# Attention by hash buckets with an MLP on one core: the first two chunks in a new order, their rows of bits copied without DMA, the dummy products on a constant

## Chip, cores and metric

The kernel runs on one core of one Trainium2 chip. The metric is the device time of one execution in microseconds (us). Before the change three runs took 306.94, 307.81 and 308.57 us; their median is 307.81 us.

## What is computed

Attention over 4 batches, 8 heads, 768 tokens and heads 64 wide, in which a query sees only the keys whose six hash bits equal its own; behind it, on 512 features a token, a norm, an MLP to 2048 and back, and a residual.

```python
B, H, S, D = q.shape                                  # 4, 8, 768, 64, float32
q_bits = (np.einsum('bhsd,dk->bhsk', q, proj) > 0)    # proj: 64 x 6
k_bits = (np.einsum('bhsd,dk->bhsk', k, proj) > 0)
mask = q_bucket[:, :, :, None] == k_bucket[:, :, None, :]   # all six bits equal
scores = np.where(mask, scale * q @ k.T, -1e9)
attn = exp(scores - max) / (sum + 1e-09)
x = (attn @ v)                                        # to [4, 768, 512]
mu, var = mean(x), mean((x - mu) ** 2)
xn = (x - mu) / np.sqrt(var + 1e-06) * g_ln
out = x + np.maximum(xn @ w_ch1, 0.0) @ w_ch2         # 512 x 2048, 2048 x 512
```

## The kernel before

**Work and tiles.** The work is cut into 12 chunks: a batch b and a third t of its tokens, 256 of them. Attention of a chunk is four pairs of heads of three units each. A unit is the scores on TensorE (`sc`, L486), their exponential on ScalarE (`ex`, L492) and the product with the values on TensorE (`av`, L506), which follows a unit or more later; after the third unit of a pair VectorE divides (`rc` and `x`, L534 to L544). The mask needs no step of its own: `slots` holds for each head the transposed tokens in rows 0 to 63 and the hash bits, as plus or minus one half, in rows 64 to 69, and the product over 70 rows is so far down where a bit differs that the exponential vanishes. `vaug` holds the values in bf16 with a column of ones.

Before the first chunk can start, the tokens of batch 0 go through a chain: loads on SyncE's queue (L147, L182), transposes in fp32 on TensorE (`tpose`, L236), their eviction to `qkT` by VectorE or ScalarE (L246, L248, L250), a cast into `slots` (L192 on ScalarE, L196 on VectorE or GpSimd), products with the projection (`hash`, L350 and L373), a comparison on VectorE that leaves `bits` (L355, L380), and the copies of the rows of bits into `slots` by `copy_by` (L189 to L196). A pair of heads has four such copies of 6 partitions x 768 (heads 0 and 1 are done apart, with copies of 6x384). Later batches are prepared otherwise: a cast on GpSimd (`nat`, L269), a DMA that transposes (L293), hashes on blocks (L312) and bits moved by DMA (L325, L331).

The MLP of a chunk is: statistics (`stats`, L564 in the first chunk) and the normed tokens on VectorE (`xn`, L572 in the first chunk, L600 later), transposes of xn on TensorE (`xnTp`, L588) with a copy to `xnT`, the first product (`hp`, L625) with its ReLU by VectorE or ScalarE (`hbuf`, L132 and L136), and the second product (`o`, L647). The weights come by DMA on GpSimd's queue (L671 and L678).

**What sets the order.** The first two chunks, and part of the attention of the third, are written out by hand under a manual schedule: each engine runs its instructions in the order in which `first_two` issues them. It reads the table `FIRST_TWO`, and `ORDER` gives the order of the units. The letters that the change touches:

- `<` is the next unit's scores and exponential, `>` the next unit's product with the values.
- `T h a` with an engine is the transposes of q (a is 0) or k (1) of head h and their eviction by VectorE (V) or ScalarE (A); `C`, `c` and `x` cast one half of the tokens, both, or the other half.
- `h` and `H` are the hash products and the bits; `r` and `B` copy the rows of bits. Of their letters the first four name the engine of each copy: V is VectorE, A ScalarE, G GpSimd, and S a DMA on SyncE's queue.
- `P`, `R` cast the values of a pair and sum them. `v`, `L`, `N`, `V`, `O`, `D`, `K`, `Q` are the loads of batch 1, its casts, its values (cast L408 and sums L415 to L417 on GpSimd), transposes, hashes, blocks and squares.
- `z` and `Z` with a number are so many dummy products of 128x128 on TensorE, whose result nobody reads (`wakep`, L799): `z` in the PSUM pool of `av`, `Z` in the general one.
- `S`, `X`, `Y`, `U` are statistics, norm, transposes and the eight steps of the first product of chunk 0's MLP; `M` is the norm of chunk 1.
- `W0` loads the first weights, `W1` and `W2` the second. `e` loads the gains of the norm (`gbc`, on SyncE), `b` makes the block-diagonal projection by eight small copies on GpSimd (L683), `p` copies the projection.

The dummy products read the tile `wake`, which VectorE clears at the start (L61 and L62). From chunk 2 on a scheduler, `interleave`, mixes the units with fillers: `plan` says which steps of the next batches' preparation come with which chunk, in up to three parts by `|`.

Of the kernel before, what the change touches and what calls it, by code (L numbers as in the profile page):

```python
# [10 lines left out]
BF16 = mybir.dt.bfloat16  # L11
# [17 lines left out]
def kernel(  # L29
# [11 lines left out]
    nc = tc.nc  # L41
    P = 128
# [15 lines left out]
    consts = ctx.enter_context(tc.tile_pool(name="consts", bufs=1))  # L58


    wake = consts.tile([P, P], BF16)  # L61
    nc.vector.memset(wake, 0.0)  # L62
    wake2 = consts.tile([P, 2], BF16)
    nc.vector.memset(wake2, 0.0)

# [682 lines left out]
    FIRST = 6  # L748
    mlp = {n: mlp_steps(*chunks[n], xs[n]) for n in range(2)}

    ORDER = "020 000 0012 0212 01 10 20 30 21 12 31 11"
    FIRST_TWO = """
p Z26 T00A T01Aa h00 C00V h01 C01A T10Aa z3 T11As e h10 r0AVVG P0 C10G C11V h11 r1VVVV < z3 < T20V T30Va < >
T21A T31V >
P1 < < H1 >
c3G >
C20A < R0 W0 T40Vs T41V >
x3V < T50V B1VSVV T51A < C21G C41G >
C40V >
< H2 P3 >  # L760
< c5G T60Va x5G T61A B2VSGS < >
P2 C61G T70V C60G T71Va < C70V >
< H3 C71G >
B3VGVG b < >
>
< R1 >
< >
W1 L0 N00 < >
< >
S0 < W2 v0 >  # L770
< >
V0 < >
S1 X0 X1 Y0V < Y1V >
< N01 U0 L1 >
< >
O0 U1 < < K011 K000 K001 >
U2 K010 Q011 U3 < >
U4 >
< D0 K100 U5 < >
< U6 >  # L780
U7 Q001 K101 K110 < Q000 K111 Q010 >
>
M
"""

    def first_two():
# [92 lines left out]

        groups = [[int(c) for c in g] for g in ORDER.split()]  # L880
        seq = [(n, 3 * j + g) for j, n, *gs in groups for g in gs or range(3)]
# [7 lines left out]
                run(op)  # L889

    plan = {
# [262 lines left out]
```

## Time and profile before

| | before |
|---|---|
| runs | 306.94, 307.81, 308.57 us; median 307.81 |
| profiled execution | 309.62 us, of which the span is 307.8 |
| mean clock granted to TensorE | 0.993 |
| busy: TensorE / its weight loads | 297.6 us (97%) / 224.1 (73%) |
| busy: ScalarE, VectorE, GpSimd | 214.4 (70%), 178.1 (58%), 92.4 us (30%) |
| DMA | 40.41 MB in 64332 packets, 131 GB/s over the span |

The page of the profile is of one execution. Its time is that of the whole execution; the span goes from the first to the last of the program's work that the profile records, and busy times and idle times lie in it. The clock is relative to full speed. An engine's idle time is put down to what released it in the end, and one that is busy 97% of the span leaves little idle time: where that lies is seen in the windows, and what ended it in the timeline, whose last column in brackets is the wait and its releaser.

### The profile page before, as it was taken

Reading aid. Unit: us, or ns where it says so; the run is one execution under the profiler, and the core shown is the slowest. Engines: PE = TensorE matmul, PEld = TensorE weight load, DVE = VectorE, ACT = ScalarE, POOL = GpSimd, SP = SyncE. Lnnn points to the kernel's source line nnn. Section 1 sums busy time; section 2 is a strip of 40 time slices with the busy share of each in tenths; the row PEclk is TensorE's granted clock in tenths of the full one; section 3 lists DMA queues with packets and bytes.
Section 4 is the critical chain, followed back from the end, with each engine's and each line's share of the span. In section 5 each row is a group of like instructions: output and inputs, shape, how many; then the busy total and the mean of one; then the engine's idle time right before and its main releaser. Section 6 shows DMA issues by size and latency. Waiting matters only on the chain.

```text
span 307.8 us, 7849 instructions
## 1 busy us (share of the span) xinstructions
PE 297.6 (97%) x3253; PEld 224.1 (73%) x3277; DVE 178.1 (58%) x401; ACT 214.4 (70%) x271; POOL 92.4 (30%) x118
## 2 busy tenths in 40 slices
PE   8998799999999999999999999999999999999995
PEld 5676478769678678669678678769679679678574
DVE  1688676853638939843874884543643633736322
ACT  4887957966878777778677867969757667676020
POOL 2667970097402524700650660200200200200100
PEclk9999979999999999999999999999999999999999
DMA  6999999058286789598385148040120110210302
GB/s 201 362 240 269 361 217 171 14 144 187 41 277 113 193 247 169 128 282 248 111 172 139 64 95 188 1 91 26 20 84 2 34 70 2 53 51 0 99 9 72
DMA packets 64332, 40.41 MB, mean 131 GB/s; under 512 B 44818, under 2 KB 60196, under 8 KB 64292
## 3 DMA queue, kind: packets, MB, share of 16 engines
q1 hardware_dynamic: 61060, 35.67, 43.7%
q0 software_dynamic: 3152, 4.19, 7.8%
q8 instruction: 26, 0.43, 0.6%
q14 instruction: 14, 0.11, 0.1%
q10 hardware_dynamic: 80, 0.00, 0.0%
HBM read 27.97 MB, written 6.88 MB: 113 GB/s over the span
## 4 chain that ended last, share of the span: by engine, by line
PE 90%; DVE 4%; ACT 2%; DMA 2%; issue 1%; DVEq 0%; ACTq 0%
PE hp L625 27%; PE o L647 26%; PE sc L486 19%; PE av L506 10%; PE hash L312 3%; DMA slots<-bits 2%; ACT ex L492 2%; PE tpose L236 1%; PE wakep L799 1%; PE hash L350 1%; DVE xn L572 1%; DVE hbuf L132 1%; DVE bt L274 1%; DVE x L544 1%; PE hash L373 1%
## 5 line engine op out<-in xcount | busy, mean ns | idle before, releaser
L492 ACT ACTIVATE ex<-sc,expb 128x1024 bf16<-128x1024 f32 x144 | 158.9, 1114 | 59.4 <-PE sc L486 59.2
L625 PE MATMUL hp<-xnT,w_sb 128*128 128x256 bf16 x768 | 98.6, 274 | 0.3 <-DVE hbuf L132 0.3
L647 PE MATMUL o<-w_sb,hbuf 128*128 128x512 bf16 (+1 forms) x376 | 92.9, 370 | 1.0
L486 PE MATMUL sc<-slots 70*128 70x256 bf16 x576 | 87.6, 273 | 0.8 <-DMA slots<-bits 0.6
L625 PEld LDWEIGHTS <-w_sb 128*128 128x128 bf16 x768 | 72.7, 98 | 10.1 <-issue 0.9
L506 PEld LDWEIGHTS <-ex 128*128 128x128 bf16 x1152 | 53.3, 97 | 18.0 <-ACT ex L492 3.4
L486 PEld LDWEIGHTS <-slots 70*128 70x128 bf16 x576 | 51.8, 97 | 15.3 <-issue 2.1
L506 PE MATMUL av<-vaug,ex 128*128 128x65 bf16 x1152 | 58.3, 193 | 1.2 <-ACT ex L492 1.0
L132 DVE TENSOR_SCALAR hbuf<-hp 128x512 bf16<-128x512 f32 x47 | 32.4, 690 | 44.2 <-PE hp L625 43.2
L647 PEld LDWEIGHTS <-hbuf 128*128 128x128 bf16 x400 | 36.9, 97 | 27.0 <-issue 0.2
L136 ACT ACTIVATE hbuf<-hp 128x512 bf16<-128x512 f32 x49 | 29.2, 595 | 19.4 <-PE hp L625 19.4
L614 POOL TENSOR_SCALAR rs<-mv 128x2 f32<-128x2 f32 x11 | 6.7, 609 | 118.4 <-DVE mv L599 118.4
L652 DVE SCALAR_TENSOR_TENSOR x<-o,rs,x 128x512 f32<-128x512 f32 (+1 forms) x25 | 18.1, 724 | 33.5 <-PE o L647 33.5
L536 DVE TENSOR_SCALAR rc<-av 128x4 f32<-128x4 f32 x36 | 5.7, 157 | 26.3 <-PE av L506 26.3
L408 POOL CAST vaug<-vnat 128x1536 bf16<-128x1536 f32 x6 | 8.8, 1470 | 40.0 <-DMA vnat<-in_v_dram 40.0
L544 DVE TENSOR_TENSOR x<-x,rc 128x256 f32<-128x256 f32 x36 | 19.6, 546 | 1.0
L600 DVE SCALAR_TENSOR_TENSOR xn<-x,mv,gbc 128x512 bf16<-128x512 f32 x22 | 15.5, 741 | 0.1
L537 DVE TENSOR_TENSOR x<-av,vsum 128x256 f32<-128x256 f32 x36 | 14.9, 414 | 0.0
L598 DVE BATCH_NORM_STATS2 stats<-x 128x6 f32<-128x512 f32 x22 | 14.1, 679 | 0.2
L269 POOL CAST nat<-qnat 128x1536 bf16<-128x1536 f32 x6 | 8.8, 1469 | 16.4 <-DMA qnat<-in_q_dram 16.3
L217 ACT ACTIVATE qnat<-qnat 128x768 f32<-128x768 f32 x16 | 13.4, 838 | 0.0
L217 ACT ACTIVATE knat<-knat 128x768 f32<-128x768 f32 x16 | 13.4, 836 | 0.0
(87 smaller groups left out, 210.9 us busy)
## 6 DMA issues: line engine op xcount, KB each, us to landing
out_dram<-x SPq DMA_DIRECT2D x23, 256.0 KB
vnat<-in_v_dram SPq DMA_DIRECT2D x7, 768.0 KB
qnat<-in_q_dram SPq DMA_DIRECT2D x11, 384.0 KB
knat<-in_k_dram SPq DMA_DIRECT2D x11, 384.0 KB
w_sb<-in_moe_w_ch_dram POOLq DMA_DIRECT2D x3, 1024.0 KB, 12.9
qnat<-in_q_dram SPq DMA_DIRECT2D x2, 768.0 KB
knat<-in_k_dram SPq DMA_DIRECT2D x2, 768.0 KB
slots<-slots SPq DMA_DIRECT2D x4, 384.0 KB
```

The lines of the kernel that those rows point to most:

```text
L132: nc.vector.tensor_scalar_max(dst, src, 0.0)
L136: nc.scalar.activation(dst, src, AF.Relu if relu else AF.Copy)
L217: done = nc.scalar.activation(src, src, AF.Square, accum_out=sq[:, a, col : col + 1])
L486: nc.tensor.matmul(sc[:, i, :], sl[0:K1, h, 1, kj * P : (kj + 1) * P], sl[0:K1, h, 0, q0 : q0 + CT],)
L492: nc.scalar.activation(ex, sc, AF.Exp, bias=expb[:, 1:2] if b else expb[:, 0:1], scale=scale if b else scale / Q_SCALE,)
L506: nc.tensor.matmul(av[:, h - ha, qi, :], state[g][:, i, qi * P : (qi + 1) * P], va[:, h, CMAP[b][kj], :], start=((g, i, qi) == (0, 0, 0)), ...
L537: nc.vector.tensor_tensor(xv, num, vs[:, ha : ha + 2, :].unsqueeze(2).to_broadcast([P, 2, TT, D]), op=AOP.add,)
L544: nc.vector.tensor_tensor(xv, num, rc.unsqueeze(3).to_broadcast([P, 2, TT, D]), op=AOP.mult)
L600: nc.vector.scalar_tensor_tensor(xn[:, :, i, :], x[:, i, :].rearrange("p (o d) -> p o d", d=P), mv[:, i, 0:1], gbc.rearrange("p (o d) -> p ...
L625: nc.tensor.matmul(hp[:, i, :], w1_sb[:, dt, nt * P : (nt + 1) * P], st["xnT"][:, dt, :], start=(dt == 0), stop=(dt == ND - 1),)
L647: nc.tensor.matmul(o2, st["h"][:, nt, i * P : (i + 1) * P], w2_sb[:, nt, cols], start=(nt == 0), stop=(nt == NH - 1),)
L652: nc.vector.scalar_tensor_tensor(x[:, i, cols], o2, st["rs"][:, i : i + 1], x[:, i, cols], op0=AOP.mult, op1=AOP.add,)
```

## The change

It has three parts.

**The constant.** `wake` is no tile any more but a constant of ones in bf16 that the program's preamble holds. The clearing of the tile by VectorE goes.

**The first two chunks.** `ORDER` and `FIRST_TWO` are written anew. No copy of a row of bits is a DMA any more: the first pair after the two single heads is copied by `VVVV` (before `VSVV`), the second by `VGGV` (`VSGS`), the third by `VVVV` (`VGVG`); head 0 by `AVVV` (`AVVG`). Casts and evictions change their engines: T00 is evicted by VectorE instead of ScalarE, T40 and T41 by ScalarE instead of VectorE; head 0 is cast whole on GpSimd (before, by halves on VectorE and ScalarE), the second half of head 1 on ScalarE (before, VectorE). The dummy products are 3 + 20 at the start and 3 later (before 26, 3 and 3), and 12 new ones stand between a unit's scores and the first transposes of xn. Pairs 1, 2 and 3 of chunk 1 now all come ahead of pair 1 of chunk 2 (before: pair 2, then pair 1 of chunk 2, then 3 and 1). `V0` stands ahead of the last statistics, `b` behind it.

**The plan of chunks 2 and 3.** Their steps are put in another order and into other parts; the steps are the same, and `o11` (GpSimd's copies of odd tokens) moves from chunk 3 to chunk 2.

```diff
-    wake = consts.tile([P, P], BF16)
-    nc.vector.memset(wake, 0.0)
+    wake = nc.const_aps.tensor(1.0, (P, P), BF16)
...
-    ORDER = "020 000 0012 0212 01 10 20 30 21 12 31 11"
+    ORDER = "000 020 0012 0212 01 10 20 30 11 21 31 12"
     FIRST_TWO = """
...
-V0 < >
-S1 X0 X1 Y0V < Y1V >
...
+W2 N00 V0 < >
+< L1 < b >
+S1 X0 N01 X1 < Z12 Y0V >
...
-        2: "o10 N11 H11 | W11 J10 T11 E10 V11 |",
-        3: "E11 o11 J11 | L20 N20 | T20 W20 O20",
+        2: "| H11 o10 E10 W11 N11 | J10 T11 o11 V11",
+        3: "J11 E11 L20 N20 T20 W20 | O20 |",
```

The lines of the changed kernel carry numbers lower by one. Where the change shows on the engines:

SyncE's queue, from the load of the last values of batch 0 on. Before, the three copies of rows of bits (`slots<-bits`) stand between the gains and the first loads of batch 1 (the second `qnat` to the last `knat`):

```order
L182 DMA vnat_139<-in_v_dram 128x4x384
L876 DMA gbc<-in_moe_g_ln_dram 128x512
L194 DMA slots_88<-bits 6x768 x3
L147 DMA qnat<-in_q_dram 128x4x384
L147 DMA knat<-in_k_dram 128x4x384
L182 DMA vnat<-in_v_dram 128x4x384
L147 DMA qnat<-in_q_dram 128x4x384
L147 DMA knat<-in_k_dram 128x4x384
```

Of the change, the same place:

```order
L181 DMA vnat_137<-in_v_dram 128x4x384
L875 DMA gbc<-in_moe_g_ln_dram 128x512
L146 DMA qnat<-in_q_dram 128x4x384
L146 DMA knat<-in_k_dram 128x4x384
L181 DMA vnat<-in_v_dram 128x4x384
L146 DMA qnat<-in_q_dram 128x4x384
L146 DMA knat<-in_k_dram 128x4x384
```

The three DMA copies are gone, and the loads of batch 1 follow the first loads directly.

VectorE, from the bits of the first pair (heads 2 and 3) to those of the third or so, before; `tpose` is an eviction, `slots<-bits` a copy of a row of bits, `rc` and `x` end a pair of chunk 0:

```order
L380 TENSOR_SCALAR bits<-hash 128x384 x2
L534 RECIPROCAL rc<-av 128x4
L544 TENSOR_TENSOR x<-av,rc 128x2x2x64
L246 TENSOR_SCALAR qkT<-tpose 128x384
L248 COPY qkT<-tpose 128x384
L196 COPY slots_88<-slots_88 64x2x384
L246 TENSOR_SCALAR qkT<-tpose 128x384
L196 COPY slots_88<-bits 6x768 x3
L534 RECIPROCAL rc<-av 128x4
L544 TENSOR_TENSOR x<-av,rc 128x2x2x64
L196 CAST slots_88<-qkT 64x2x384
L380 TENSOR_SCALAR bits<-hash 128x384 x2
```

And in the change:

```order
L379 TENSOR_SCALAR bits<-hash 128x384 x2
L533 RECIPROCAL rc<-av 128x4
L543 TENSOR_TENSOR x<-av,rc 128x2x2x64
L195 COPY slots_86<-bits 6x768 x4
L245 TENSOR_SCALAR qkT<-tpose 128x384
L247 COPY qkT<-tpose 128x384
L533 RECIPROCAL rc<-av 128x4
L543 TENSOR_TENSOR x<-av,rc 128x2x2x64
L379 TENSOR_SCALAR bits<-hash 128x384 x2
L195 COPY slots_86<-slots_86 64x2x384
L245 TENSOR_SCALAR qkT<-tpose 128x384
L195 COPY slots_86<-bits 6x768 x2
```

Four copies of bits stand now right behind the first division, ahead of the next evictions; before, two evictions and a copy of odd tokens stood ahead of them. The cast (64x2x384) is no longer in this stretch.

GpSimd, from the last casts of batch 0 to the values of batch 1 (`vaug` and `vsum`), before; `proj` are the eight small copies of `b`, `w_sb` the loads of the second weights, `nat` a cast of batch 1:

```order
L196 CAST slots_88<-qkT 64x2x384 x3
L196 COPY slots_88<-bits 6x768 x2
L683 COPY proj_83<-proj_62 32x6 x8
L678 DMA w_sb<-in_moe_w_ch_dram 128x8x512
L678 DMA w_sb<-in_moe_w_ch_dram 128x4x512
L269 CAST nat_653<-qnat 128x4x384
L678 DMA w_sb<-in_moe_w_ch_dram 128x4x512
L408 CAST vaug_91<-vnat 128x24x64
L415 TENSOR_TENSOR vsum_94<-vaug_91 128x256
L417 TENSOR_TENSOR vsum_94<-vsum_94,vaug_91 128x256 x3
L417 TENSOR_TENSOR vs_731<-vsum_94,vaug_91 128x256
```

And in the change:

```order
L195 CAST slots_86<-qkT 64x2x384
L677 DMA w_sb<-in_moe_w_ch_dram 128x8x512
L677 DMA w_sb<-in_moe_w_ch_dram 128x4x512 x2
L268 CAST nat_677<-qnat 128x4x384
L407 CAST vaug_89<-vnat 128x24x64
L414 TENSOR_TENSOR vsum_92<-vaug_89 128x256
L416 TENSOR_TENSOR vsum_92<-vsum_92,vaug_89 128x256 x3
L416 TENSOR_TENSOR vs_680<-vsum_92,vaug_89 128x256
L682 COPY proj_81<-proj_60 32x6 x8
L268 CAST nat_677<-knat 128x4x384
```

The two copies of bits are no longer here, and the eight small copies stand behind the values instead of ahead of them.

More of the change, by code (lines that the diff above doesn't have):

```diff
@@ L749 @@
     mlp = {n: mlp_steps(*chunks[n], xs[n]) for n in range(2)}
-    ORDER = "020 000 0012 0212 01 10 20 30 21 12 31 11"
+    ORDER = "000 020 0012 0212 01 10 20 30 11 21 31 12"
     FIRST_TWO = """
[L753 to L764, printed above, removed]
->
-< R1 >
-< >
[L768 to L771, printed above, removed]
-V0 < >
-S1 X0 X1 Y0V < Y1V >
[L774 to L781, printed above, removed]
+z3 Z20 T00V p T01Aa c0G h00 h01 T10As x0G T11As h10 r0AVVV C11A h11 < r1VVVV < z3 e C10G T20V P0 T30V < P1 T21Va T31V >
+< >
+C31G C20V H1 C30G < W0 >
+< >
+T40As >
+B1VVVV T41A R0 c4A T50Va x4G < T51V < >
+c5G H2 C21G < >
+x5V T60Va T61A < P3 B2VGGV C60G T70V >
+< >
+T71A < >
+C70G >
+C61V L0 P2 < C71G H3 B3VVVV < >
+< >
+R1 >
+v0 < S0 W1 >
+< < >
+>
+W2 N00 V0 < >
+< L1 < b >
+S1 X0 N01 X1 < Z12 Y0V >
+Y1V >
+< U0 U1 < >
+< >
+K011 U2 K001 < U3 >
+U4 < O0 >
+< K000 U5 >
+K010 U6 >
+K101 K100 < D0 Q011 < >
+Q001 < U7 >
 >
-M
+Q000 K110 K111 Q010 M
 """
```

## Prediction

> **What bounds the kernel now.** I read the page from the top: busy time by engine, the slices, the chain that ended last.
>
> ```profile
> PE 297.6 (97%) x3253; PEld 224.1 (73%) x3277; DVE 178.1 (58%) x401; ACT 214.4 (70%) x271; POOL 92.4 (30%) x118
> PEclk9999979999999999999999999999999999999999
> PE 90%; DVE 4%; ACT 2%; DMA 2%; issue 1%; DVEq 0%; ACTq 0%
> ```
>
> TensorE holds 90% of the chain and is busy 297.6 of 307.8 us, so only 307.8 - 297.6 = 10.2 us are left in which it stands, and one slice in which its clock is not whole. The edit touches the order of the first two chunks, so the question is how much of this lies there. The view by windows says so:
>
> ```profile
> 0.00:10.00 10.00, 8.68 (x61) 5.54 (x62) 3.45 (x11) 4.81 (x8) 3.72 (x17) 1.00 0.74 224
> 20.00:30.00 10.00, 8.89 (x133) 6.05 (x133) 8.75 (x18) 8.04 (x9) 7.39 (x9) 1.00 1.08 241
> 30.00:40.00 10.00, 7.14 (x98) 4.86 (x97) 6.82 (x16) 8.03 (x10) 9.37 (x17) 1.00 1.09 345
> 50.00:60.00 10.00, 9.95 (x134) 7.57 (x132) 7.66 (x15) 7.85 (x12) 0.00 (x0) 1.00 0.46 78
> 60.00:70.00 10.00, 9.95 (x106) 6.38 (x106) 6.01 (x12) 7.41 (x13) 7.57 (x6) 1.00 0.50 124
> ```
>
> The columns are length, busy PE, PEld, DVE, ACT, POOL, clock, DMA share, GB/s. TensorE stands 1.3 us in the first ten, 1.1 us from 20 to 30, 2.9 us from 30 to 40, and 0.05 us in each later row shown: from 50 us on it is work alone. A microsecond won before 50 us is therefore won at the end, since what follows is the same work in a row; and nothing else can be won.
>
> **Term B, the waits from 22 to 29 us.** The timeline gives each stall with what ended it:
>
> ```profile
> 22.52 0.31 PEld L236 LDWEIGHTS tpose<-identf,qnat 128*128 128x128 f32 x3 [0.43 <-PE sc L486]
> 23.43 0.31 PEld L236 LDWEIGHTS tpose<-identf,knat 128*128 128x128 f32 x3 [0.60 <-DVE bits L380]
> 24.77 0.38 PE L486 MATMUL sc<-slots 70*128 70x256 bf16 x2 [0.57 <-DMA slots<-bits]
> 28.56 0.11 PEld L486 LDWEIGHTS <-slots 70*128 70x128 bf16 x2 [0.19 <-DMA slots<-bits]
> ```
>
> Two of the four wait for rows of bits that SyncE copies by DMA (the "S" places of B1 and B2); the chain of waits shows the first copy whole:
>
> ```profile
> 19.12 5.61 DMA slots<-bits
> ```
>
> A few rows of bits take 5.61 us, because the DMA engines are full there (share 1.08 in the row 20 to 30). The change has no such copy: its B1 is four DVE copies, B2 two DVE and two GpSimd, B3 four DVE. The price of a copy, one alone and then the group:
>
> ```profile
> 19.61 0.38 DVE L196 COPY slots<-bits 6x768 bf16<-6x768 bf16 x1
> L196 DVE COPY slots<-bits 6x768 bf16<-6x768 bf16 x6 | 4.0, 662 | 0.2
> L196 DVE COPY slots<-bits x12: 252/366/886, 7.9 to 29.6; 6x384 bf16<-6x384 bf16 x6, 6x768 bf16<-6x768 bf16 x6
> L196 DVE CAST slots<-qkT x4: 543/600/1023, 6.3 to 27.1; 64x768 bf16<-64x768 f32 x4
> ```
>
> DVE gets four more copies of 6x768 (ten for six) and one more of 6x384, and loses two casts of 64x768: 4 x 0.38 + 0.25 - 2 x 0.60 = +0.6 us at best, 4 x 0.886 + 0.45 - 2 x 0.543 = +2.9 us at worst (0.45 is my estimate between the least and the greatest of that group). The rows of B1 were 5.61 us under way; four copies at the mean of 0.66 are 2.6 us. The two DMA waits go whole. The other two (bits L380 holds the PSUM tile that the next transposes want; DVE was 8.75 busy of 10 us) shrink where the change sends evictions to ScalarE (T40 and T41 by "A") and grow where DVE has more to copy. The DMA waits alone are 0.57 + 0.19 = 0.8 us; all TensorE idle time of that row is 1.1; by the weight loads, whose idle time has no modelled tail, 0.43 + 0.60 + 0.57 + 0.19 = 1.8, which is the upper end. If DVE slips, term B is 0. **I take -1.2.**
>
> [...]
>
> **Term C, the first norm, 36 to 41 us.** Here TensorE stands longest:
>
> ```profile
> 36.77 1.48 POOL L408 CAST vaug<-vnat 128x1536 bf16<-128x1536 f32 x1
> 36.98 1.82 DVE L572 SCALAR_TENSOR_TENSOR xn<-x,mv,gbc 128x512 bf16<-128x512 f32 x1
> 38.33 0.95 POOL L415 TENSOR_TENSOR vsum<-vaug 128x256 f32<-128x256 bf16 x1
> 38.96 0.87 DVE L572 SCALAR_TENSOR_TENSOR xn<-x,mv,gbc 128x512 bf16<-128x512 f32 x1
> 38.86 0.40 PE L588 MATMUL xnTp<-ident,xn 128*128 128x128 bf16 x4 [1.46 <-DVE xn L572]
> 39.89 0.40 PE L588 MATMUL xnTp<-ident,xn 128*128 128x128 bf16 x4 [0.19 <-DVE xn L572]
> L600 DVE SCALAR_TENSOR_TENSOR xn<-x,mv,gbc x22: 732/744/751, 60.0 to 284.8; 128x512 bf16<-128x512 f32 x22
> ```
>
> The first xn takes 1.82 us beside GpSimd's cast of V; the second, beside sums, 0.87; the same shape later 0.74. In the change V0 stands ahead of the last statistics, and on GpSimd ahead of the eight copies of b and behind fewer rows of bits:
>
> ```profile
> 31.24 1.75 POOL L683 COPY proj<-proj 32x6 f32<-32x6 f32 x8
> 29.35 1.84 POOL L196 COPY slots<-bits 6x768 bf16<-6x768 bf16 x2 [0.88 <-DVE bits L380]
> ```
>
> So V's cast comes 1.75 + 1.84 = 3.6 us sooner and ends near 36.77 + 1.48 - 3.6 = 34.7, before the norm; the sums lie beside xn then, and xn costs 0.87: 0.95 us less. The queue of TensorE gains too: the scores and twelve dummy products stand ahead of the first transposes, so that the wait is partly filled (at most 12 x 0.11 = 1.3 us of it, by the three at 10.03 below). Bounds: 0 if the cast still meets xn, -1.6 (1.46 + 0.19) if all waiting goes. **C1 is -0.9.**
>
> Then the clock, in two stretches:
>
> ```profile
> 36.00:40.00 4.00, 1.98 (x28) 1.25 (x25) 3.83 (x7) 2.14 (x3) 3.84 (x5) 1.00 1.14 292
> 40.00:45.00 5.00, 5.00 (x51) 3.97 (x50) 3.01 (x7) 2.65 (x3) 4.59 (x7) 0.66 1.24 214
> 41.11 1.91 PE L625 MATMUL hp<-xnT,w_sb 128*128 128x256 bf16 x8
> 44.35 1.04 PE L625 MATMUL hp<-xnT,w_sb 128*128 128x256 bf16 x8
> ```
>
> In the four thin microseconds TensorE works 1.98 of 4; in the five behind them the mean clock is 0.66, so 5 x 0.34 = 1.7 us of work are lost; eight products of one kind take 1.91 us in it and 1.04 behind it. With the wait shortened and dummies in it, I expect no such dip: **C2 is -1.7.** If it comes all the same, C2 is 0.
>
> [...]
>
> **Terms A and D, the start and the later table.** The start is held by transfers:
>
> ```profile
> 1.22 2.95 PE L799 MATMUL wakep<-wake 128*128 128x128 bf16 x26 [1.22 <-DVE wake L62]
> 4.83 0.50 PEld L236 LDWEIGHTS tpose<-identf,knat 128*128 128x128 f32 x3 [0.43 <-DMA knat<-in_k_dram]
> 4.84 0.90 PE L236 MATMUL tpose<-identf,knat 128*128 128x128 f32 x3
> 7.18 0.55 PE L236 MATMUL tpose<-identf,qnat 128*128 128x128 f32 x3
> 10.03 0.33 PE L799 MATMUL wakep<-wake 128*128 128x128 bf16 x3
> ```
>
> The constant is there before the cleared tile, but that wins nothing: the K tile lands at 4.83 whatever the dummies do, and three dummies fewer (23 for 26, at 2.95 / 26 = 0.11 us) end sooner into the same wait. A is 0, between -0.2 and +0.3. (The three at 10.03 take 0.33 / 3 = 0.11 us each, tail and all: the price used above.) D, the reordered rows for chunks 2 and 3: TensorE has no idle time in these rows, the moved steps lie mostly on SyncE and GpSimd, of which GpSimd has 2.4 of ten free (7.57 busy from 60 to 70); 0, within 0.3 either way, since the loads, casts and hashes moved are the same ones.
>
> What it adds: ScalarE takes over two evictions of 128x384 and one whole cast, beside exponentials that fill it; no row shows what of it TensorE waits for, so +0.2, between 0 and +0.6.
>
> **The sum** against the profiled execution: -1.2 - 0.9 - 1.7 + 0 + 0 + 0.2 = **-3.6 us**, 309.62 to 306.0; against the median of the runs shown, 307.81 - 3.6 = **304.2**. The profiled execution is 1.8 us above that median; I carry the difference over. That difference is the part of the execution outside the span (309.62 - 307.8), as far as this trace can tell. All ends together reach from -1.8 - 1.6 - 1.7 - 0.2 - 0.3 = -5.6 to 0.3 + 0.3 + 0.6 = +1.2.
>
> **The rivals.**
> *The clock dips anyway.*
>
> ```profile
> 31.46 6.47 ACT L492 ACTIVATE ex<-sc,expb 128x1024 bf16<-128x1024 f32 x6
> ```
>
> For it: exponentials back to back pace 31 to 38 us and still will, TensorE is thin there, and how thin is too thin no row tells. Against: that stretch was thin before and the clock stayed whole in it; it fell only behind the four microseconds that were half empty. B and C1 stay: -3.6 + 1.7 = -1.9, time 305.9. Chance 0.14.
> *The clock rises late at the start.* The products at 4.84 take 0.90 us and their like at 7.18 0.55, so the array is slow until about 6 us; with fewer dummies and an emptier opening it could stay slow one stretch longer. A stretch of half clock as long as the one above is worth 1.7 at full use, of which waits hide a part; I estimate +1.5, time 305.7. Chance 0.12.
> *DVE becomes the bound.* It has 10 - 8.75 = 1.25 us free from 20 to 30 and could get +2.9: 1.65 late on the path, no B, no C1 as the norm comes later: -1.7 + 0.2 + 1.65 = +0.15, time 308.0. Against: the two stretches ahead of it have room (the next row is 6.82 busy). Chance 0.08.
> *Slower: the first weights come late.* Without SyncE's copies the loads of the next batch go out straight behind the first ones, and the weights of W0 share with them:
>
> ```profile
> 14.42 1.75 POOL L671 DMA_DIRECT2D w_sb<-in_moe_w_ch_dram  x2
> 25.35 0.44 SPq L147 DMA_DIRECT2D qnat<-in_q_dram  x1
> w_sb<-in_moe_w_ch_dram POOLq DMA_DIRECT2D x3, 1024.0 KB, 12.9
> 0.00:45.00 45.00, 39.71 (x470) 28.83 (x471) 28.82 (x66) 32.49 (x38) 30.92 (x54) 0.96 1.03 277
> ```
>
> Five loads of 768 KB (3.9 MB) that went out from 25.35 us on would now go out at about 10 to 16, by estimate: behind the last first-batch load, and behind the two GpSimd casts that free the tile of V. The first batch is 4.7 MB, W0 puts 2.1 MB. If the engines served all else first, W0 would land after 10.7 MB: 39 us at the 277 GB/s of the first 45 us, 44.5 us at the 241 of the row 20 to 30, in which W0 was moved. The first hp product, now at 41.11, wants it at about 41.11 - 2 = 39. So the price is 0 to 5.5 us; at its end 307.81 - 3.6 + 5.5 = 309.7. It decides from a landing of 39 + 3.6 = 42.6 us on. Against: two queues share the engines, and under a share of 1.08 the landing took 12.9 us from an issue at 14.42, which leaves over 10 us of room. Chance 0.08.
>
> **How the numbers follow.** The forecast has the remaining 0.58. About 0.5% (1.5 us) is what a measurement of this kernel can tell from no change. Faster by more: forecast, both clock cases, 0.58 + 0.14 + 0.12 = 0.84; the same: DVE, 0.08; slower: 0.08, though part of it would be within 0.5%; I give 0.83, 0.10, 0.07. The range leaves out the last two rivals: low is 307.81 - 5.4 = 302.4 (B, C1 and C2 at their ends, A and D -0.3 together), high 306.6, the clock rivals with 0.7 for their own bounds.
>
> **What would show it.** B: no DMA slots<-bits in the chain, DVE copies of bits x10 of 6x768 at 0.4 to 0.7 us, TensorE over 9.4 us busy from 20 to 30. C1: first xn under 1.2 us and V's cast ended before it. C2: granted clock 1.00 in every stretch from 30 to 50 us. A: first transposes of K still at 4.8. D: 9.95 busy from 60 to 80. A wait of hp for w_sb, or of TensorE for DVE rows near 29 us, or a clock of 0.5 past 7 us would make it wrong.

## The result, and the profile after

The changed kernel takes 305.85 us in the median of 14 executions (304.98 to 308.12), the kernel before beside it 308.48 us in the median of 14. The ratio is 0.9938, 95% interval 0.9918 to 0.9958: about 1.9 us less; the two medians lie 2.6 us apart. The forecast was 3.6 us less. The direction is right, the size is half to three quarters. The ratios, here and below, leave out executions more than 1.5% above the fastest of their kernel (713.64, 345.69, 313.47, 312.25 and 311.73 us), and the medians, means and counts below leave out the first two of these.

The two profiled executions differ by just the forecast: 309.62 us before, 306.01 us after, spans 307.8 and 304.5. So this one pair agrees with the prediction, and the executions that nobody profiled don't. That is the puzzle of this case.

The page of the changed kernel, its busy times, its granted clock by slices and its chain:

```profile
PE 296.2 (97%) x3283; PEld 224.3 (74%) x3283; DVE 177.8 (58%) x403; ACT 213.7 (70%) x271; POOL 92.4 (30%) x118
PEclk9999999999999999999999999999999999999999
PE 91%; DVE 3%; ACT 2%; DMA 1%; issue 1%; POOL 1%; SPq 0%; DVEq 0%; ACTq 0%; POOLq 0%
```

TensorE is idle for 304.5 - 296.2 = 8.3 us (before 10.2), and no slice in mid-span has a clock below whole. The same windows as before (length, busy PE, PEld, DVE, ACT, POOL, clock, DMA share, GB/s):

```profile
0.00:10.00 10.00, 8.04 (x59) 5.13 (x60) 3.03 (x11) 4.36 (x8) 4.99 (x18) 1.00 0.73 221
20.00:30.00 10.00, 9.33 (x150) 7.44 (x135) 9.47 (x18) 9.24 (x11) 9.63 (x12) 1.00 1.10 252
30.00:40.00 10.00, 8.79 (x124) 7.42 (x123) 6.88 (x20) 8.47 (x8) 3.92 (x4) 1.00 1.13 262
40.00:50.00 10.00, 10.00 (x148) 8.72 (x145) 7.12 (x13) 7.86 (x10) 6.54 (x16) 1.00 1.29 218
60.00:70.00 10.00, 10.00 (x98) 7.76 (x97) 5.66 (x8) 6.06 (x9) 8.79 (x8) 1.00 0.93 188
```

TensorE is 0.6 us less busy in the first ten, 0.4 more from 20 to 30 and 1.65 more from 30 to 40, and the clock is whole from 40 to 50, where it had been 0.83 in the kernel before:

```profile
40.00:50.00 10.00, 10.00 (x114) 8.49 (x113) 6.64 (x13) 7.65 (x10) 4.68 (x7) 0.83 1.25 196
```

The prediction had asked for over 9.4 us of work from 20 to 30 us; it is 9.33. The copies of rows of bits on VectorE, as a group (least, median and greatest duration in ns, first and last start):

```profile
L195 DVE COPY slots<-bits x17: 251/353/868, 7.6 to 29.5; 6x768 bf16<-6x768 bf16 x10, 6x384 bf16<-6x384 bf16 x7
```

They are ten and seven, as the prediction counted, and TensorE still has one wait for them, in the timeline:

```profile
29.49 0.61 PE L485 MATMUL sc<-slots 70*128 70x256 bf16 x4 [0.67 <-DVE slots L195]
```

A wait of TensorE for these copies near 29 us was one of the signs by which the prediction said it would be wrong. At 0.67 us it is no shorter than the DMA's wait of 0.57 us in the profile of before.

Now the norm. The timeline of GpSimd and VectorE shows both xn at 0.75 us, as hoped, but for another reason than the one in the prediction:

```profile
37.94 1.47 POOL L407 CAST vaug<-vnat 128x1536 bf16<-128x1536 f32 x1 [5.96 <-DMA vnat<-in_v_dram]
...
35.51 0.75 DVE L571 SCALAR_TENSOR_TENSOR xn<-x,mv,gbc 128x512 bf16<-128x512 f32 x1
36.42 0.75 DVE L571 SCALAR_TENSOR_TENSOR xn<-x,mv,gbc 128x512 bf16<-128x512 f32 x1
```

V's cast did not end before the norm; it began behind it, at 37.94, because GpSimd stood 5.96 us until V of batch 1 had landed.

### The profile page after: what moved, and what is told of

It reads as the page before. It is cut to its first block, busy times and chain, and to the rows that moved or that the text cites. A ratio compares the mean times of both kernels' runs of the same rounds, so it can differ in the third digit from the quotient of the medians.

```text
span 304.5 us, 7881 instructions
## 1 busy us (share of the span) xinstructions
PE 296.2 (97%) x3283; PEld 224.3 (74%) x3283; DVE 177.8 (58%) x403; ACT 213.7 (70%) x271; POOL 92.4 (30%) x118
## 4 chain that ended last, share of the span: by engine, by line
PE 91%; DVE 3%; ACT 2%; DMA 1%; issue 1%; POOL 1%; SPq 0%; DVEq 0%; ACTq 0%; POOLq 0%
PE hp L624 28%; PE o L646 27%; PE sc L485 19%; PE av L505 10%; PE hash L311 3%; ACT ex L491 2%; DVE slots L195 2%; PE tpose L235 1%; DMA knat<-in_k_dram 1%; PE hash L349 1%; POOL slots L195 1%; PE av L520 0%; DVE qkT L245 0%; DVE bits L379 0%; PE wakep L798 0%
## 5 line engine op out<-in xcount | busy, mean ns | idle before, releaser
L646 PE MATMUL o<-w_sb,hbuf 128*128 128x512 bf16 (+1 forms) x400 | 96.2, 370 | 0.9 <-issue 0.9
L543 DVE TENSOR_TENSOR x<-x,rc 128x256 f32<-128x256 f32 x36 | 18.2, 505 | 1.0
```

Of the source, the lines that this page charges most:

```text
L543: nc.vector.tensor_tensor(xv, num, rc.unsqueeze(3).to_broadcast([P, 2, TT, D]), op=AOP.mult)
L646: nc.tensor.matmul(o2, st["h"][:, nt, i * P : (i + 1) * P], w2_sb[:, nt, cols], start=(nt == 0), stop=(nt == NH - 1),)
```

## The experiments

Each execution reports its span and its mean granted clock. One stretch at half clock as long as that in the profile of before (3.41 us, from 40.69 on) costs 0.0055 of the mean; so an execution with 0.997 or more had its clock whole from its first rise to the last products, and one with 0.994 or less had it fall in mid-span. "Fell" counts the latter; how late the clock rose at the start this mean does not show (the profiled execution of after_warmer, in which three transposes at 8.93 us still take 0.85 us, has 1.0). Ratios are to the kernel before, run beside the kernel on the same chip. It was run in four sets: the first beside after_again, after_warmer, before_fill12 and after_nofill, the second beside after_late_v, before_late_v, before_rows and after_late_v_nofill, the third beside before_rows_late_v, before_fill12_again and after_lvn_dma_rows, the fourth beside late_v_nofill_again.

| kernel | median us | ratio, 95% interval | fell | median where whole |
|---|---|---|---|---|
| before, in four sets | 308.15, 308.56, 307.65, 308.57 | | 18/31, 23/27, 17/29, 10/16 | 307.13, 306.59, 306.81, 306.77 |
| the change | 305.85 | 0.9938 [0.9918, 0.9958] | 0/14 | 305.85 |
| after_again | 306.31 | 0.9946 [0.9912, 0.998] | 3/12 | 305.75 |
| after_warmer | 305.64 | 0.9905 [0.9867, 0.9943] | 2/8 | 305.42 |
| before_fill12 | 308.17 | 0.9999 [0.9974, 1.0024] | 1/13 | 308.09 |
| after_nofill | 305.55 | 0.9929 [0.9897, 0.9962] | 5/12 | 304.93 |
| after_late_v | 305.42 | 0.9929 [0.9893, 0.9965] | 0/8 | 305.42 |
| before_late_v | 305.97 | 0.9938 [0.9909, 0.9968] | 1/12 | 305.90 |
| before_rows | 307.19 | 0.9963 [0.9941, 0.9985] | 2/12 | 307.19 |
| after_late_v_nofill | 304.87 | 0.9903 [0.9872, 0.9934] | 1/8 | 304.81 |
| before_rows_late_v | 307.23 | 0.9969 [0.9939, 1.0] | 0/12 | 307.24 |
| before_fill12_again | 308.13 | 1.0021 [0.9984, 1.0057] | 1/10 | 307.98 |
| after_lvn_dma_rows | 306.62 | 0.9958 [0.9921, 0.9996] | 5/12 | 305.30 |
| late_v_nofill_again | 305.22 | 0.9916 [0.9884, 0.9948] | 3/12 | 305.03 |

### Do executions differ, and in what

**after_again**, the changed kernel unaltered.

> The changed kernel once more. Theory 1 (the change is worth its 3.6 us only against executions of before in which the clock falls near 41 us, and this falls out in part of them): this kernel's own runs lie close together, within 1 us, the first hp product starts at 38.3 us within 0.3, and the gap to before is 2 to 3 us. Theory 2 (the emptier opening of the changed kernel lets the clock rise late in some of its executions): its runs spread over 2 to 3 us, with some 1.5 us or more above the fastest; in such an execution the first products are at half speed until after 6.5 us and the first hp product starts after 39 us.

Measured: 305.03 to 308.80 us, a spread of 3.8 us. The change's own clock can fall too (3 of 12). And the profile of this execution is another one at the norm:

```profile
36.04 1.47 POOL L407 CAST vaug<-vnat 128x1536 bf16<-128x1536 f32 x1 [4.13 <-DMA vnat<-in_v_dram]
...
36.35 1.72 DVE L571 SCALAR_TENSOR_TENSOR xn<-x,mv,gbc 128x512 bf16<-128x512 f32 x1
...
38.12 0.40 PE L587 MATMUL xnTp<-ident,xn 128*128 128x128 bf16 x4 [0.82 <-DVE xn L571]
```

V landed 1.9 us earlier than in the first profile, its cast began just ahead of the second xn, xn took 1.72 us instead of 0.75, and TensorE waited 0.82 us for it. So neither theory had the whole: the spread was larger than theory 1 allowed, and the signs of theory 2 are there (three transposes at 4.21 us take 0.89 us and eight hash products at 5.06 take 1.86, where those at 5.02 and 5.50 in the first profile take 0.55 and 1.49; and the first hp product came at 39.14). But the late rise is not what delayed it: the first xn started at 35.44, against 35.51 in the first profile, in which the clock rose at 4.05. The cause that this profile shows is a third one, when V lands.

**after_warmer**, with dummies in the waits of the opening.

```diff
-z3 Z20 T00V p T01Aa c0G h00 h01 T10As x0G T11As h10 r0AVVV C11A h11 < r1VVVV < z3 e C10G T20V P0 T30V < P1 T21Va T31V >
+Z23 T00V p T01Aa c0G z3 h00 h01 z3 T10As x0G z3 T11As z3 h10 r0AVVV C11A h11 < r1VVVV < z3 e C10G T20V P0 T30V < P1 T21Va T31V >
```

> The changed kernel with 12 more dummy products in the waits of the opening (23 ahead of the first transposes as before, and three each ahead of h00, of the transposes of head 1 and of h10). Theory 2: the clock rises in the same stretch in every execution, so the slowest runs go and the median falls by 0.4 to 1.2 us against the changed kernel. Theory 1: nothing but the dummies' own time where the waits don't cover it, 0 to +0.5 us against the changed kernel.

Measured: a median of 305.64, hardly below the change's (305.85 and 306.31), and executions up to 308.25 us are still there. The profiled one was that one, and it shows the late rise all the same. Transposes of head 1 in its opening:

```profile
7.97 0.85 PE L235 MATMUL tpose<-identf,qnat 128*128 128x128 f32 x3
8.61 0.53 PE L798 MATMUL wakep<-const-bfloat16-1.0 128*128 128x128 bf16 x3
8.93 0.85 PE L235 MATMUL tpose<-identf,knat 128*128 128x128 f32 x3
```

and the same ones in after_again:

```profile
6.86 0.55 PE L235 MATMUL tpose<-identf,qnat 128*128 128x128 f32 x3
7.24 0.49 PE L235 MATMUL tpose<-identf,knat 128*128 128x128 f32 x3
```

The three at 8.93 us take 0.85 us, where those of after_again at 7.24 take 0.49; and three dummies at 9.57 take 0.53 us, against 0.34 at 12.02: by these the clock rose only near 10 us. The rival of a late rise is real (this span is 306.6 us), but more dummies didn't cure it; how often it comes is not settled.

### The dummy products

**before_fill12** puts twelve dummies into the wait of 1.46 us and changes nothing else (C2 alone).

```diff
-S1 X0 X1 Y0V < Y1V >
+S1 X0 X1 Z12 Y0V < Y1V >
```

> The kernel before with 12 dummy products ahead of the first transposes of xn, where TensorE waited 1.46 us; all else as it was. If the clock fell near 41 us for want of work in that wait (my term C2), it stays whole there, and the time falls by 1.7 us against before, or by less in the mean if only a part of the executions of before had the fall: 0.5 to 1.2 us. If the fall has another cause, the granted clock still shows a half stretch after 40 us, and the time is within 0.5 us of before.

> before_fill12 once more, for an execution whose clock stays whole. There the clock fell in 1 of 13 executions, against 18 of 31 of before beside it, and yet the time was that of before. Theory 1 (the dummies fill a wait that stays as long, and their 0.8 us are free): xn's wait after the dummies is 0.4 to 0.8 us, and the first hp product starts at 41.0 to 41.4 us as in the profile of before. Theory 2 (in executions with a shorter wait the dummies themselves are late): the transposes of xn follow the dummies with no wait, and the dummies end 0.5 us or more after xn was ready.

Measured: the clock fell in 1 of 13 and 1 of 10 executions, where that of before beside them fell in 18 of 31 and 17 of 29. So work in that wait does keep the clock up. Yet the time is that of before, twice (0.9999 and 1.0021). The profile of the first is its one execution with a fall, and that lies elsewhere, at 25.57 us, within a wait for a row of bits by DMA; its timeline, and a window of it:

```profile
25.99 0.59 PE L486 MATMUL sc<-slots 70*128 70x256 bf16 x2 [1.96 <-DMA slots<-bits]
```

```profile
25.00:30.00 5.00, 4.01 (x31) 3.48 (x31) 2.26 (x5) 1.65 (x2) 2.92 (x4) 0.56 1.07 283
```

In the profile of before this wait was 0.57 us. The second run's profile shows the dummies with no wait behind them:

```profile
37.70 0.83 PE L799 MATMUL wakep<-wake 128*128 128x128 bf16 x12
38.36 0.39 PE L588 MATMUL xnTp<-ident,xn 128*128 128x128 bf16 x4
```

There xn took 0.77 us and was ready at 38.21, so the dummies were in the way, by some 0.2 us only (its theory 2, but not the 0.5 us). Executions of before with a whole clock take 307.13 and 306.81 us, those with dummies 308.09 and 307.98. One reason may be, and isn't shown, that the clock of before stays whole mainly in executions whose wait is short, so that the two groups differ in more than the clock. The profiles of this repeat and of before_late_v (below), both with a whole clock, show where 2.6 us of difference in the span lie: 0.7 us by the first xn of chunk 1 (57.73 against 57.00), 0.8 us more by that of chunk 11 (282.20 against 280.69), where TensorE waits 0.61 us for hbuf at 118.90, and 1.1 us at the very end, where TensorE stands 0.97 us at 301.85 for nothing that the profile shows. The last two lie far behind the dummies; whether these have a part in them isn't settled.

**after_nofill** takes the dummies out of the change.

```diff
-S1 X0 N01 X1 < Z12 Y0V >
+S1 X0 N01 X1 < Y0V >
```

> The changed kernel without the 12 dummy products ahead of the first transposes of xn. Theory 1 as forecast (the wait for xn is short by now, so that nothing is left to fill): the clock stays whole, and the time is 0 to 0.7 us less, since 12 products of 0.06 us are gone. Rival (the dummies carry C2): a stretch at half clock between 38 and 48 us is back in the profile or in some runs, and the time is 0.5 to 1.7 us more than that of the changed kernel.

Measured: signs of both, neither clear of the noise. Where the clock stays whole it is 0.8 to 0.9 us faster (304.93 against 305.85 and 305.75), and the clock falls more often (5 of 12 against 3 of 26); the ratios are the same within their intervals. Its profile had the collision again, V landing earlier still:

```profile
35.73 1.47 POOL L407 CAST vaug<-vnat 128x1536 bf16<-128x1536 f32 x1 [4.21 <-DMA vnat<-in_v_dram]
...
35.96 1.79 DVE L571 SCALAR_TENSOR_TENSOR xn<-x,mv,gbc 128x512 bf16<-128x512 f32 x1
...
37.80 0.40 PE L587 MATMUL xnTp<-ident,xn 128*128 128x128 bf16 x4 [1.30 <-DVE xn L571]
```

### V's cast and the norm

**after_late_v**: GpSimd's cast of V and of K behind the transposes of xn, so that it can't meet them whenever V lands.

```diff
-W2 N00 V0 < >
+W2 N00 < >
...
-S1 X0 N01 X1 < Z12 Y0V >
-Y1V >
+S1 X0 X1 < Z12 Y0V >
+Y1V > N01 V0
```

> The changed kernel with V0 and N01 (GpSimd's cast and sums of the values and its cast of K of batch 1) behind the transposes of xn, so that neither can lie beside the norm, whenever V lands. Theory of the landing (the change put V0 ahead of the norm, but the cast waits for V's DMA, which lands anywhere from 35 to 38 us, and costs the second xn 0.9 to 1.0 us wherever they meet): both xn take 0.75 us in every execution, the first hp product starts at 38.3 to 38.6 us with an early clock, and the mean falls by 0.5 to 0.9 us against the changed kernel. Rival (the clock's rise at the start makes the spread, not the landing): no change within 0.3 us.

Measured: 305.42, no fall in 8, 7 of them between 304.98 and 305.67 and one at 308.28. Both xn take 0.75 us, the first hp product starts at 37.67, and V's cast at 38.86 without any wait. The mean is 305.71 us, against 306.14 and 306.55 of the change: 0.4 to 0.8 us less, about as the theory of the landing has it, but the intervals of the ratios overlap.

**before_late_v**: the same in the kernel before, one step moved.

```diff
-V0 < >
-S1 X0 X1 Y0V < Y1V >
+< >
+S1 X0 X1 Y0V < Y1V > V0
```

> The kernel before with V0 behind the transposes of xn; no dummies added, all else as it was. If GpSimd's cast beside xn made TensorE's wait of 1.46 us, and that wait makes the clock fall in about half the executions, then xn takes 0.75 us, the wait goes under 0.6 us, runs with one half stretch go, and the mean falls by 1.5 to 2 us against before. If the wait comes from elsewhere (the statistics, the division ahead of it), it stays over 1 us and the time is within 0.5 us of before.

Measured: 305.97 against 308.56, ratio 0.9938, as much as the whole change gains, by one moved step. The clock fell in 1 of 12 instead of 23 of 27. Its norm:

```profile
39.37 1.45 POOL L408 CAST vaug<-vnat 128x1536 bf16<-128x1536 f32 x1
...
36.85 0.75 DVE L572 SCALAR_TENSOR_TENSOR xn<-x,mv,gbc 128x512 bf16<-128x512 f32 x1
...
37.76 0.75 DVE L572 SCALAR_TENSOR_TENSOR xn<-x,mv,gbc 128x512 bf16<-128x512 f32 x1
...
37.66 0.40 PE L588 MATMUL xnTp<-ident,xn 128*128 128x128 bf16 x4 [0.40 <-DVE xn L572]
```

The wait of 1.46 us is 0.40: GpSimd's cast beside xn made it, and that wait made the clock fall.

**after_late_v_nofill** leaves out the twelve dummies as well, and **late_v_nofill_again** repeats it.

```diff
-S1 X0 X1 < Z12 Y0V >
+S1 X0 X1 < Y0V >
```

> As after_late_v, without the 12 dummy products ahead of the transposes of xn. Without the collision there is no long wait, so the clock should stay whole without them, and 12 products of 0.06 to 0.07 us are saved where they aren't covered: 0 to -0.7 us against after_late_v. Rival (thin work from 30 to 38 us lets the clock fall anyway): runs with a half stretch are back, and the mean is 0.3 to 1 us higher.

> after_late_v_nofill once more, since it is the candidate to beat both kernels. If its gain over the changed kernel (305.0 against 306.1 and 306.6 us in the mean) is real, the mean is again 304.7 to 305.5 us and the ratio to before at most 0.993; if it was a lucky set of executions, the mean is that of the changed kernel, 306 us or more.

Measured: medians of 304.87 and 305.22, ratios 0.9903 and 0.9916. With V out of the way the medians are 0.2 to 0.6 us lower without the dummies (305.42 with them), within the intervals; the clock can still fall (4 of 20), as the rival said. The repeat's profile is such an execution; two windows of it:

```profile
27.00:31.00 4.00, 2.86 (x39) 2.30 (x36) 3.81 (x10) 3.15 (x5) 3.96 (x5) 1.00 1.11 252
31.00:38.00 7.00, 6.89 (x69) 5.57 (x67) 3.60 (x10) 5.82 (x6) 3.12 (x12) 0.51 1.13 262
```

It beats the kernel before clearly, by 3.0 and 2.6 us by the ratios. Both its medians lie under both of the changed kernel (305.85 and 306.31), but their intervals to before overlap, and the two were not run side by side.

### The rows of bits

**before_rows**: the letters alone, in the order of before (term B alone).

```diff
-x3V < T50V B1VSVV T51A < C21G C41G >
+x3V < T50V B1VVVV T51A < C21G C41G >
...
-< c5G T60Va x5G T61A B2VSGS < >
+< c5G T60Va x5G T61A B2VGGV < >
...
-B3VGVG b < >
+B3VVVV b < >
```

> The kernel before with the rows of bits by VVVV, VGGV and VVVV and no copy by DMA; all else as it was (term B alone). As forecast: -1.2 us, with no wait for slots from DMA. Theory of the spread (a row's landing can be 1.4 us later than in the profile of before, and the clock can fall behind that): the runs of before with two half stretches go, and the mean falls by 0.8 to 1.8 us. Rival (VectorE becomes the bound): 0 to +1 us, with TensorE waiting for VectorE's copies between 22 and 30 us.

Measured: 307.19 against 308.56; the means are 307.09 and 308.29, a difference of 1.2 us, just what the prediction gave for B, but not by B: GpSimd lost the two copies of the third pair as well (and got one more of the second), so its cast of V came sooner and met less of the norm:

```profile
35.48 1.46 POOL L408 CAST vaug<-vnat 128x1536 bf16<-128x1536 f32 x1
...
37.62 0.75 DVE L572 SCALAR_TENSOR_TENSOR xn<-x,mv,gbc 128x512 bf16<-128x512 f32 x1
...
38.52 0.92 DVE L572 SCALAR_TENSOR_TENSOR xn<-x,mv,gbc 128x512 bf16<-128x512 f32 x1
```

**before_rows_late_v**: with the collision out of the way in both.

Its diff is that of before_rows and that of before_late_v together.

> The kernel before with both single edits: no row of bits by DMA (VVVV, VGGV, VVVV) and V0 behind the transposes of xn. before_rows alone was 1.2 us under before and before_late_v alone 2.1 us. Theory 1 (term B is a gain of its own, from the waits for DMA of 0.57 and 0.19 us): 3.0 to 3.3 us under before. Theory 2 (most of the gain of before_rows came by GpSimd, which without its two copies of bits cast V sooner, so that it met the norm less): no better than before_late_v within 0.5 us, as the collision can be removed only once, and TensorE waits for VectorE near 22 us instead of for DMA near 24.

Measured: 307.23, 1.3 us more than before_late_v in the median and 1.0 more by the ratios to before, so theory 2 and more: in the order of before, the copies on VectorE cost more than the DMA's waits. VectorE is the bound there, busy 9.69 of the ten us from 20 to 30. The waits of TensorE, two of them for VectorE, and the window:

```profile
22.59 0.52 PE L236 MATMUL tpose<-identf,qnat 128*128 128x128 f32 x3 [1.00 <-PE sc L486]
23.47 0.55 PE L236 MATMUL tpose<-identf,knat 128*128 128x128 f32 x3 [0.36 <-DVE bits L380]
26.67 0.42 PE L506 MATMUL av<-vaug,ex 128*128 128x65 bf16 x8 [0.77 <-DVE x L544]
```

```profile
20.00:30.00 10.00, 7.87 (x118) 5.36 (x107) 9.69 (x19) 6.96 (x8) 7.15 (x10) 1.00 1.10 252
```

**after_lvn_dma_rows**: the other way, three rows by DMA again in after_late_v_nofill.

```diff
-B1VVVV T41A R0 c4A T50Va x4G < T51V < >
+B1VSVV T41A R0 c4A T50Va x4G < T51V < >
...
-x5V T60Va T61A < P3 B2VGGV C60G T70V >
+x5V T60Va T61A < P3 B2VSGS C60G T70V >
```

> after_late_v_nofill with three rows of bits by DMA again, at the places of before (VSVV and VSGS): term B undone in the changed order, without collision and without dummies. Theory 1 (term B is a gain of its own): +0.8 to +1.5 us against after_late_v_nofill, with TensorE waiting for slots from DMA and some runs with a fallen clock. Theory 2 (VectorE's four copies cost as much as the DMA's waits): within 0.4 us of after_late_v_nofill.

Measured: 306.62 against 304.87; the means are 306.44 against 305.01, and against 305.51 in late_v_nofill_again, so the DMA's copies cost 0.9 to 1.4 us here: 0.3 to 0.5 us where the clock stays whole (305.30 against 304.81 and 305.03), and the rest by falls (5 of 12 against 4 of 20, too few to be sure of). The wait, on the weight loads of the scores; on their matmuls it is 1.19 us:

```profile
27.70 0.11 PEld L485 LDWEIGHTS <-slots 70*128 70x128 bf16 x2 [1.47 <-DMA slots<-bits]
```

## Why the prediction was half right

**Term B (-1.2) held, in the changed order.** Undone there it costs 0.9 to 1.4 us in the mean. But the prediction added it up from waits alone, and with a whole clock these bring 0.3 to 0.5 us; the rest may come by falls behind such waits, which it had not priced, so that the size is in part luck. The wait that the DMA makes (before the matmuls of the scores) is not always the 0.57 us of the profile: it was 1.19 and 1.96 us in others. It is not a gain of the letters alone: in the order of before they cost 1.0 to 1.3 us, by the mechanism of the rival "DVE becomes the bound". The new order, with evictions on ScalarE and other units between, is what makes room for them; which of its steps does was not tried.

**Term C1 (-0.9) failed, and here is the step.** The prediction said that V's cast "comes 1.75 + 1.84 = 3.6 us sooner and ends near 36.77 + 1.48 - 3.6 = 34.7, before the norm". It took GpSimd's queue, which did hold the cast in the kernel before, for all that could hold it, and didn't ask when V lands. Three profiles of kernels with this order and no change to the opening have GpSimd idle, 4 to 6 us, until that landing: at 37.94, 36.04 and 35.73 us. The norm lies from 35 to 37 us, so that the cast, freed of its queue, falls onto the second xn in two of the three (1.72 and 1.79 us for 0.75). A wait in a queue had been traded for a wait for a transfer. The load of V itself goes out 13 us sooner in the change, as the prediction saw under its rival of the late weights; SyncE's issues of it before and after are

```profile
26.37 0.51 SPq L182 DMA_DIRECT2D vnat<-in_v_dram  x1
...
12.98 1.63 SPq L181 DMA_DIRECT2D vnat<-in_v_dram  x1
```

Yet it landed no sooner: after 25 us in the profile of the change, with the DMA engines full (share 1.10 from 20 to 30 and 1.13 from 30 to 40), where in that of before V had landed 10.4 us after its issue or sooner, since GpSimd began its cast at 36.77 without a wait for it. On the path of TensorE the collision costs 1.0 us, about as priced: from the first xn of chunk 0 to the first of chunk 1 it is 20.72 us in the profile of the change, 21.68 in after_again and 21.75 in after_nofill. Moving V behind the norm in the kernel before brings, by itself, 1.9 us by the ratio, as much as the whole change.

The collision itself is measured: xn takes 0.75 us with GpSimd idle (the profile of the change) and 1.72 to 1.82 us beside GpSimd's cast of 1.47 to 1.48 us (after_again, after_nofill, before, before_fill12).

**Term C2 (-1.7) was right in its mechanism and wrong as a size.** One fall costs what the prediction said: from the first xn of chunk 0 to the first of chunk 1 it is 22.99 us in the profile of before and 21.30 in that of before_fill12, both with the collision (xn 1.82 and 1.78 us) and only the former with the fall. The dip is gone in 23 of 26 executions of the change. But it was never in every execution of before: its clock fell in 68 of 103 and stayed whole in 35. Against its executions with a whole clock (medians of 306.59 to 307.13) the change's 305.85 and 305.75 win 0.7 to 1.4 us, where the prediction has 1.9 us without C2. In before the mean of all executions lies 1.1 to 1.7 us above that of the whole ones (308.20 against 307.14, 308.29 against 306.58, 308.18 against 306.77), in the change 0 to 0.5 us. So the falls are worth about 1.2 us in the mean by this estimate, not 1.7, and they come at waits for DMA (before_fill12, at 25.57) as well as behind the norm. The profiled execution of before had a fall and a clock that rose late (three transposes at 4.84 still take 0.90 us); that of the change had neither (0.55 us at 5.02) and was spared the collision. That is how one pair shows 3.6 us and the medians 2.6 or less.

The prediction read why the clock falls from a single fall. The four falls in mid-span are at 40.69 us in before, 25.57 in before_fill12, 24.35 in before_rows and 31.18 in late_v_nofill_again, and the clock then stays at half for 3.4 us (before, where it is 3.41, and before_rows) or 6.8 us (before_fill12, late_v_nofill_again). TensorE is far from idle ahead of them: in late_v_nofill_again, from 27 to 31 us, it worked 2.86 of 4 us, and the clock fell at 31.18. How thin is too thin, which the prediction said no row tells, the traces together don't give as one number. In the 3.41 us ahead of the four falls TensorE was busy 1.76, 1.33, 2.04 and 2.28 us; yet in after_nofill it was busy 1.72 of the 3.41 us from 34.39 on, in before_rows_late_v 2.05 of those from 20.06 on, and the clock stayed whole in both. So how much work is missing does not by itself decide whether a wait makes a fall. What else does wasn't shown; in before the fall lies 34.13 us behind the first rise at 6.56, ten times the 3.41 us that it lasted, and that the place of a wait in such steps matters is the author's estimate from that.

**The sum was read from one execution and taken off another.** The prediction saw that the profiled execution lay 1.8 us above the median of the three and carried its terms over whole, calling the difference "the part of the execution outside the span". Every execution on record has 1.5 to 1.9 us outside its span, that of the change too (306.01 and 304.5), so that explains nothing. What made this execution longer than the others stayed open, and with it which of its terms the median execution has: the fall, 1.7 of the 3.6 us, is in 68 of 103. That the pair then came out at 3.6 is luck: at the first xn of the last chunk the two are 4.6 us apart (284.11 and 279.50), and 1.3 us of it are lost in the last 25 us, where in the execution of the change TensorE stands 0.91 us at 299.58 for nothing that the profile shows. Nor is it "work alone" from 50 us on: from the first xn of chunk 1 to the end of the span the profiles of all the runs here take from 247.0 to 249.3 us.

**What it added (+0.2) left out the dummies.** Twelve of them were priced at nothing, as a fill for a wait. The profiles agree, even without the collision: from the first xn of chunk 0 to that of chunk 1 it is 20.71 us in after_late_v and 20.72 in after_late_v_nofill. The medians (305.42 with them, 304.87 and 305.22 without) leave it open.

**Terms A and D.** The first transposes of K began at 5.02 us in the profile of the change, after a wait of 0.71 us for K's landing, and at 4.21 in that of after_again, against 4.84 before; no run has A alone, and nothing here speaks against 0. TensorE is busy 10.00 of 10 us from 60 to 70, so nothing is waited for in D's stretch. The weights' rival did not come as such: the first hp product started at 38.26 with no wait for w_sb. Its premise came true (the loads of batch 1 go out from 10.85 us on, before from 25.35), but it was V, not the weights, that an engine waited for.

Most of what the forecast hoped for is there once V is moved: after_late_v_nofill takes 3.7 us less than before in the medians (304.87 against 308.56) and 3.3 us in the repeat, 3.0 and 2.6 us by the ratios.

## What to carry to other kernels

A step that is moved ahead in its engine's queue can still stand until the last of its inputs is there, as V's cast did here for 4.13 to 5.96 us: before the queue's time is booked as a gain, look for the landing of the transfer that feeds it, and see what it would meet then. A term read from one execution (a fallen clock, a DMA's landing) needs the share of executions that have it; the span and the mean clock of each execution give that without a second profile. A gain that is read from an execution well above the median can be taken off the median only when it is known what made that execution long. And where a change does several things, the one step that carries the gain may be the one that it did only halfway.

## What the hardware showed

- The clock can fall when TensorE is far from idle: in the 3.41 us ahead of the four falls in mid-span it was busy 1.33 to 2.28 us, while with 1.72 us in after_nofill and 2.05 us in before_rows_late_v the clock stayed whole. Its first rise comes at different times: at 6.56 us in the profile of before and at 4.05 in that of the change, and in after_warmer three transposes at 8.93 us still take 0.85 us.
- The same copies of a few rows by DMA let the matmuls of the scores wait up to 0.57 us in the profile of before and up to 1.96 us in that of before_fill12, which has the same copies.
- The copies of rows of bits (six partitions x 384 or 768 elements) take 0.35 us on VectorE in the median and up to 0.87 us; GpSimd, which could take them too, is busy 9.63 of the ten us from 20 to 30 in the change.
- A cast of 1.47 us on GpSimd cost the xn beside it 1.0 us, and TensorE up to 1.30 us in the changed order and 1.46 in that of before.
